# Bilinear layer: output products of two feature pairs in one PSUM group, and work moved between VectorE and GpSimd

## The chip, the cores and the metric

The kernel runs on one core of a Trainium2 chip. The metric is the time of one execution in microseconds of the device, median of three runs. Before the change it is 724.49 us (724.02 to 724.53).

## The reference

Three layers follow one another; the 1152 tokens are 2 batches of 576.

```python
# attention: 2 batches, 8 heads, 576 tokens, 64 columns a head
scores = scale * np.matmul(q, k.transpose(0, 1, 3, 2))
cum = np.cumsum(np.maximum(s, 0.0), axis=-1)
bias = -(cum[:, :, :, None] - cum[:, :, None, :])
scores = np.where(causal, -1000000000.0, scores + np.minimum(bias, 0.0))
x = softmax(scores) @ v                      # as 1152 x 512
# four experts, 512 -> 1024 -> 512, weighted by shares p
for e in range(E):
    h = np.maximum(x @ w1[e], 0.0)
    out += p[:, e:e + 1] * (h @ w2[e])
# bilinear layer, 512 -> 1536 -> 512
a = out @ w_a
b = out @ w_b
return (a * b @ w_out).astype(np.float32)
```

(The softmax is shortened here; all is float32.)

## The kernel before

**Precision.** Every float32 factor is kept as two parts: a high part, which ScalarE copies (L80), and a low part, which another engine makes by a subtraction (L81). A product is three matmuls, high by high, high by low and low by high (`mm3`, L281). In the program's names a trailing h or l is the part: `wh`, `wl` are weights, `h2h`, `h2l` the features between two layers, `tqh`, `tql` sums of input quarters.

**Stages.** To about 200 us attention runs with the first expert beside it. Then come three relu experts to about 480 us, a turn of the sum `acc` into the input `x` of the last layer, and from about 505 us the bilinear layer. Its 1536 features are worked off in six stages, m = 0 to 5, of one feature pair each (two blocks of 128). A stage multiplies the 1152 tokens by the pair's `wa` and then by its `wb`. 896 of the tokens go through `quadrants`, which forms seven products of quarters instead of eight, with sums of weight quarters (`sums`, made at L189 to L192) and of input quarters; each product is 128 x 448. The other 256 tokens go directly (`pst`). `keep_b` multiplies a by b in PSUM (L1202) and splits the result into `h2h` and `h2l`. Then the output tiles follow: nine tiles of 128 tokens by 512 columns, each six matmuls with the pair's half of `wo` (`second_pair`). The first stage copies a tile to `acc` on ScalarE (L1223), the others add it on VectorE (L1225), and the last one sends it out (L1227); the very last tile is done in two halves of 256 columns (`last_tile`, L1213).

**Weights.** `wa`, `wb` and `wo` come as 64-bit numbers. A piece is loaded by a DMA on SyncE's queue into one of three `raw` buffers and made into float32 by `narrow`: an Abs on ScalarE (L161), a max and min on GpSimd (L162), and three bit operations on VectorE (L166, L170, L174). Two such pieces make a wide pair (`tp`), one a piece of `wo` (`t`); there is one buffer of each. `split_pair` then makes the four sums on GpSimd and both low parts, of the quarters themselves (`wl<-tp`) and of the sums (`wl<-sums`), on GpSimd too, each one instruction of 128 x 1024. A wide piece of `wo` has its low part of 128 x 512 on GpSimd. For the experts' weights, which come as float32, the sums stand on VectorE and the low parts on GpSimd. Three places hold pairs, two hold halves of `wo` (or of the experts' second weights), and two pairs of `h2h`, `h2l` stand at a time.

**Order.** The program emits units of work one after another, and a clock of assumed costs says when a weight piece is loaded and split beside them; the pieces stand in a list: `wa` and `wb` of a stage with the `wo` of the stage before between them. `pipelined` lets the output tiles of a stage stand beside the products of the next. A scheduler then orders each engine's instructions by a simulated timeline; on the chip each engine works off its list in order and waits at semaphores. Products use five PSUM banks, output tiles three.

## Time and profile before

| | |
|---|---|
| time, median of three runs | 724.49 us (724.02 to 724.53) |
| profiled execution: its time, its span | 725.65 us, 723.9 us |
| TensorE matmul busy | 710.9 us, 98% of the span |
| VectorE busy | 512.9 us, 71% |
| GpSimd busy | 398.8 us, 55% |
| ScalarE busy | 323.5 us, 45% |
| TensorE's granted clock | 1.00 throughout |

A matmul's end is modelled and reaches into the next one, so the starts are the thing to read: where two of them lie further apart than the columns need, TensorE stood still. In a row of the timeline the bracket at its end is the engine's idle time before the instruction and what ended it. PE is TensorE, DVE VectorE, ACT ScalarE, POOL GpSimd, and SPq SyncE's queue that issues DMAs.

### The profile page before, as it was taken

The numbers are of one execution on the slowest core, as the hardware profiler recorded it, in microseconds if no ns is written. First come the engines' busy times: TensorE is split into PE (matmuls) and PEld (weight loads), VectorE is DVE, ScalarE is ACT, GpSimd is POOL, SyncE is SP. The second block draws the span as 40 slices with busy tenths as digits, with TensorE's granted clock in tenths as the row PEclk, the third lists the DMA queues.
The fourth block names the chain that finished last, engine by engine and source line by source line (L and its number), as shares of the span: only waits on it lengthen the run. The fifth ranks groups of instructions, "written<-read, shape, count | busy, mean of one in ns | idle before, by whom it ended". The sixth has DMA issues, their size and how long they took to land.

```text
span 723.9 us, 10979 instructions
## 1 busy us (share of the span) xinstructions
PE 710.9 (98%) x3884; PEld 620.9 (86%) x3886; DVE 512.9 (71%) x1060; ACT 323.5 (45%) x722; POOL 398.8 (55%) x329
## 2 busy tenths in 40 slices
PE   9999999999999999999999999999999999999998
PEld 5886798999899888888888888887999888888886
DVE  5586878767686866765655666589973969787674
ACT  3597899877434333331223123334544424243410
POOL 5476866655235544430333057687277879788600
PEclk9999999999999999999999999999999999999999
DMA  8665434442111211120111021222021222212003
GB/s 328 209 176 141 126 88 119 124 120 62 57 41 58 89 58 58 59 65 24 58 59 47 13 88 59 88 87 88 30 87 59 88 88 83 92 60 88 1 0 131
DMA packets 33724, 61.42 MB, mean 85 GB/s; under 512 B 3285, under 2 KB 17525, under 8 KB 33669
## 3 DMA queue, kind: packets, MB, share of 16 engines
q1 hardware_dynamic: 33189, 59.61, 26.6%
q10 hardware_dynamic: 480, 1.11, 0.4%
q8 instruction: 31, 0.51, 0.3%
q14 instruction: 24, 0.20, 0.1%
HBM read 55.11 MB, written 2.58 MB: 80 GB/s over the span
## 4 chain that ended last, share of the span: by engine, by line
PE 76%; DVE 9%; POOL 5%; issue 4%; ACT 4%; DMA 3%; SPq 0%; POOLq 0%; ACTq 0%; DVEq 0%
PE ps L281 34%; PE psq L281 24%; PE pst L281 6%; PE av L702 2%; PE tr L670 2%; POOL wl L81 2%; PE ps L1037 2%; DMA raw<-in_wo 1%; DVE el L686 1%; DVE tp L174 1%; PE lullps L736 1%; ACT e L651 1%; DVE h2l L81 1%; DVE tp L170 1%; POOL tp L162 1%
## 5 line engine op out<-in xcount | busy, mean ns | idle before, releaser
L281 PE MATMUL ps<-wh,h2h 128*128 128x512 f32 (+1 forms) x334 | 131.1, 392 | 0.6 <-ACT h2h L80 0.6
L281 PE MATMUL ps<-wl,h2h 128*128 128x512 f32 (+1 forms) x334 | 129.9, 389 | 0.0
L81 POOL TENSOR_TENSOR wl<-raw,wh 128x1024 fp32r<-128x1024 f32 x24 | 58.2, 2433 | 129.0 <-ACT wh L80 98.6
L281 PE MATMUL ps<-wh,h2l 128*128 128x512 f32 (+1 forms) x334 | 125.6, 390 | 0.0
L335 DVE SCALAR_TENSOR_TENSOR acc<-ps,pr,acc 128x512 f32<-128x512 f32 x111 | 82.3, 746 | 41.1 <-PE ps L281 40.4
L281 PE MATMUL psq<-xh,wh 128*128 128x448 f32 (+1 forms) x224 | 81.7, 365 | 0.1
L281 PE MATMUL psq<-xh,wl 128*128 128x448 f32 (+1 forms) x224 | 81.4, 363 | 0.0
L281 PE MATMUL psq<-xl,wh 128*128 128x448 f32 (+1 forms) x224 | 81.3, 363 | 0.0
L281 PEld LDWEIGHTS ps<-wh,h2l 128*128 128x128 f32 x334 | 62.7, 188 | 13.2
L281 PEld LDWEIGHTS ps<-wh,h2h 128*128 128x128 f32 x334 | 62.8, 188 | 13.0 <-ACT h2h L80 1.3
L346 ACT ACTIVATE h2h<-psq 128x448 fp32r<-128x448 f32 (+1 forms) x56 | 29.5, 530 | 95.5 <-PE psq L281 76.4
L281 PEld LDWEIGHTS ps<-wl,h2h 128*128 128x128 f32 x334 | 62.8, 188 | 10.9
L81 POOL TENSOR_TENSOR wl<-sums,wh 128x1024 fp32r<-128x1024 f32 x24 | 58.3, 2427 | 4.9 <-ACT wh L80 4.9
L80 ACT ACTIVATE wh<-raw 128x1024 fp32r<-128x1024 f32 x24 | 25.5, 1062 | 69.6 <-PE ps L281 53.0
L281 PE MATMUL psq<-tqh,wh 128*128 128x448 f32 x144 | 53.0, 368 | 1.3 <-DVE h2l L81 0.9
L281 PE MATMUL psq<-tql,wh 128*128 128x448 f32 x144 | 52.6, 365 | 0.0
L281 PE MATMUL psq<-tqh,wl 128*128 128x448 f32 x144 | 52.5, 364 | 0.0
L162 POOL TENSOR_SCALAR tp<-tp 128x512 f32<-128x512 f32 x24 | 48.0, 2017 | 5.8 <-ACT tp L161 5.8
L686 DVE TENSOR_TENSOR el<-tr,eh 128x512 fp32r<-128x512 f32 (+5 forms) x80 | 38.3, 484 | 16.4 <-ACT eh L685 15.6
L659 POOL TENSOR_SCALAR e<-e,r 128x448 f32<-128x448 f32 (+4 forms) x64 | 37.8, 595 | 17.5 <-DVE r L658 12.9
L281 PEld LDWEIGHTS psq<-xh,wh 128*128 128x128 f32 x224 | 42.1, 188 | 4.3 <-ACT s L445 0.9
L281 PEld LDWEIGHTS psq<-xl,wh 128*128 128x128 f32 x224 | 42.1, 188 | 3.5
(205 smaller groups left out, 1877.2 us busy)
## 6 DMA issues: line engine op xcount, KB each, us to landing
raw<-in_w SPq DMA_DIRECT2D x32, 512.0 KB
raw<-in_wa SPq DMA_DIRECT2D x12, 512.0 KB
raw<-in_wb SPq DMA_DIRECT2D x12, 512.0 KB
raw<-in_wo SPq DMA_DIRECT2D x12, 512.0 KB
kr<-in_kT SPq DMA_DIRECT2D x16, 288.0 KB
w<-in_w SPq DMA_DIRECT2D x8, 512.0 KB
vr<-in_v SPq DMA_DIRECT2D x16, 160.0 KB
kb<-ks SPq DMA_DIRECT2D x16, 144.0 KB
```

What stands on the lines that cost most here:

```text
L80: nc.scalar.activation(out=hi, in_=src, func=AF.Copy)
L81: lo_eng.tensor_tensor(out=lo, in0=src, in1=hi.bitcast(F32), op=ALU.subtract)
L162: nc.gpsimd.tensor_scalar(out=t.bitcast(F32), in0=t.bitcast(F32), scalar1=2.0**-15, scalar2=GMAX, op0=ALU.max, op1=ALU.min,)
L170: nc.vector.scalar_tensor_tensor(out=t, in0=lo, scalar=29, in1=t, op0=ALU.logical_shift_right, op1=ALU.bitwise_or,)
L281: ins = nc.tensor.matmul(ps, lhsT=l, rhs=r, start=first and k == 0, stop=last and k == 2, skip_group_check=more)
L335: nc.vector.scalar_tensor_tensor(out=dst, in0=ps, scalar=share, in1=dst, op0=ALU.mult, op1=ALU.add)
L346: nc.scalar.activation(out=hh, in_=src, func=AF.Relu)
L659: nc.gpsimd.tensor_scalar(out=t.e, in0=t.e, scalar1=r, scalar2=1.0, op0=ALU.mult, op1=ALU.mult)
L670: ins = nc.tensor.transpose(ps[:, c - c0, :], t.e[:, k0 : k0 + P], ident)
L686: nc.vector.tensor_tensor(out=j.el[:, c0:c1, x], in0=src, in1=hi.bitcast(F32), op=ALU.subtract)
L702: ins = nc.tensor.matmul(ps[:, o:], lhsT=j.vs[:, c, :], rhs=e[:, c, o:], start=(m == 0), stop=(m == len(mms) - 1),)
L1037: ins = nc.tensor.matmul(ps, lhsT=w, rhs=x, start=start, stop=stop)
```

## The change

It has three parts. `split` can make its low part in several slices (`less`), and GpSimd makes those of pairs and of the experts' second weights in two halves: 60 instructions of 128 x 1024 become 120 of 128 x 512. The low parts of `wo` (12 instructions of 128 x 512) and the sums of wide pairs (48 of 128 x 256) move from GpSimd to VectorE. And the output products of stages m-1 and m, m odd, are summed in PSUM: a tile is one group of twelve matmuls, with nine tiles behind every odd stage and none behind an even one. With m = 1 ScalarE copies a tile to `acc`, with m = 3 and 5 VectorE adds it, so that of 44 additions of 512 columns 17 are left. The order of tiles is 7, 8, 0 to 6, and the last one is done in two halves. In the list of pieces the two `wo` of a couple of stages now stand together, between `wa` and `wb` of the next even stage.

```diff
@@ split
-    def split(hi, lo, src, lo_eng):
+    def split(hi, lo, src, lo_eng, parts=1):
         nc.scalar.activation(out=hi, in_=src, func=AF.Copy)
-        lo_eng.tensor_tensor(out=lo, in0=src, in1=hi.bitcast(F32), op=ALU.subtract)
+        less(lo, src, hi, lo_eng, parts)
+
+    def less(lo, src, hi, eng, parts):
+        n = lo.shape[1] // parts
+        for k in range(parts):
+            x = slice(k * n, k * n + n)
+            eng.tensor_tensor(out=lo[:, x], in0=src[:, x], in1=hi[:, x].bitcast(F32), op=ALU.subtract)
@@ split_pair, split_piece
-        split(*direct, r.rearrange("p c (i f) -> p i c f", i=2), nc.gpsimd)
-        split(wh[:, 8:], wl[:, 8:], sums, nc.gpsimd)
+        split(*direct, r.rearrange("p c (i f) -> p i c f", i=2), nc.gpsimd, 2)
+        split(wh[:, 8:], wl[:, 8:], sums, nc.gpsimd, 2)
...
-            split(wh[:, j, :], wl[:, j, :], t.bitcast(F32), nc.gpsimd)
+            split(wh[:, j, :], wl[:, j, :], t.bitcast(F32), nc.vector)
         elif form == "half":
-            split(wh, wl, r, nc.gpsimd)
+            split(wh, wl, r, nc.gpsimd, 2)
...
-                split_pair(key, t.bitcast(F32), nc.gpsimd)
+                split_pair(key, t.bitcast(F32), nc.vector)
@@ the list of pieces
-    for m in range(NTH * NPR):
-        queue_pair(("wa", m), wa[m // NPR], m % NPR, True)
         if m:
-            queue_half(("wo", m - 1), wo[(m - 1) // NPR], (m - 1) % NPR, True)
-        queue_pair(("wb", m), wb[m // NPR], m % NPR, True)
-    queue_half(("wo", m), wo[m // NPR], m % NPR, True)
+    for m in range(0, NTH * NPR, 2):
+        queue_factor("wa", wa, m)
+        if m:
+            queue_out(m - 2)
+            queue_out(m - 1)
+        queue_factor("wb", wb, m)
+        queue_factor("wa", wa, m + 1)
+        queue_factor("wb", wb, m + 1)
+    queue_out(m)
+    queue_out(m + 1)
@@ ab_stage
+        both = (m - 1, m)
+        order = [7, 8, *range(7)]
+
+        def products(ps, t, n):
+            for k, (mo, i) in enumerate((mo, i) for mo in both for i in range(2)):
+                mm3(
+                    ps, cols(hts["g", mo], i, slice(t, t + P)), cols(slabs["wo", mo], i, n),
+                    k == 0, k == 3,
+                )
...
         def tile_of(t):
+            last = (m, t) == (NTH * NPR - 1, order[-1] * P)
+            for n in (slice(0, DM // 2), slice(DM // 2, DM)) if last else (slice(0, DM),):
+                ps = ps_m.tile([P, n.stop - n.start], F32, tag="mm", name="ps2")
+                products(ps, t, n)
                 dst = acc[:, t // P, n]
+                if m == 1:
+                    nc.scalar.activation(out=dst, in_=ps, func=AF.Copy)
+                else:
+                    nc.vector.tensor_tensor(out=dst, in0=ps, in1=dst, op=ALU.add)
+                if m == NTH * NPR - 1:
+                    nc.sync.dma_start(out=out[t : t + P, n], in_=dst)
...
-        o = [(("wo", m), T1, lambda t=t: tile_of(t)) for t in range(0, NT, P)]
+        keys = tuple(("wo", mo) for mo in both)
+        o = [(keys, 2 * T1, lambda t=t * P: tile_of(t)) for t in order] if m % 2 else []
```

In the rows of the changed program a line of the kernel stands six or more lines further down: L81 has become L87, L162 L168, L166 L172, L170 L176, L174 L180, L189 to L192 L195 to L198, L281 L287, L436 L442, and L1202 L1218.

**GpSimd, in the third stage.** Before, one wide pair with the piece of `wo` and the next pair's first two pieces behind it:

```order
L162 TENSOR_SCALAR tp<-tp 128x512 x2
L190 TENSOR_TENSOR sums<-tp 128x256
L189 TENSOR_TENSOR sums<-tp 128x256
L191 TENSOR_TENSOR sums<-sums,tp 128x256
L81 TENSOR_TENSOR wl<-tp,wh 128x1024
L192 TENSOR_TENSOR sums<-tp,sums 128x256
L162 TENSOR_SCALAR t<-t 128x512
L81 TENSOR_TENSOR wl<-sums,wh 128x1024
L162 TENSOR_SCALAR tp<-tp 128x512 x2
```

After the change; the first `t<-t` here is the one whose shift stands second in VectorE's list below:

```order
L168 TENSOR_SCALAR tp<-tp 128x512 x2
L87 TENSOR_TENSOR wl<-tp,wh 128x512 x2
L87 TENSOR_TENSOR wl<-sums,wh 128x512 x2
L168 TENSOR_SCALAR t<-t 128x512
L168 TENSOR_SCALAR tp<-tp 128x512 x2
L168 TENSOR_SCALAR t<-t 128x512
L87 TENSOR_TENSOR wl<-tp,wh 128x512 x2
L87 TENSOR_TENSOR wl<-sums,wh 128x512 x2
```

The sums are gone from here, each subtraction stands as two halves, and the halves of the quarters and of the sums stand one behind the other, four in a row, with no other instruction between them. The max and min of a piece of `wo` stood between the two subtractions of a pair; now it stands behind all four halves.

**VectorE, in the third stage, at the split of the 256 direct tokens (`h2l<-pst`).** Before:

```order
L1202 TENSOR_TENSOR pst<-pst,sr 128x512
L1202 TENSOR_TENSOR psq<-psq,u_6208 128x448
L166 TENSOR_SCALAR t<-t 128x512
L81 TENSOR_TENSOR h2l<-pst,h2h 128x2x256
L170 SCALAR_TENSOR_TENSOR t<-raw,t 128x512
L81 TENSOR_TENSOR h2l<-psq,h2h 128x448
L174 SCALAR_TENSOR_TENSOR t<-raw,t 128x512
L436 TENSOR_TENSOR psq<-psq,s_6409 128x448
L1202 TENSOR_TENSOR psq<-psq,s_6206 128x448
L166 TENSOR_SCALAR tp<-tp 128x512
L436 TENSOR_TENSOR psq<-psq,u_6410 128x448
L170 SCALAR_TENSOR_TENSOR tp<-raw,tp 128x512
```

After:

```order
L442 TENSOR_TENSOR psq<-psq,u_6417 128x448
L172 TENSOR_SCALAR t<-t 128x512
L1218 TENSOR_TENSOR pst<-pst,sr 128x512
L1218 TENSOR_TENSOR psq<-psq,u_6182 128x448
L176 SCALAR_TENSOR_TENSOR t<-raw,t 128x512
L172 TENSOR_SCALAR tp<-tp 128x512
L87 TENSOR_TENSOR h2l<-pst,h2h 128x2x256
L442 TENSOR_TENSOR psq<-psq,s_6415 128x448
L180 SCALAR_TENSOR_TENSOR t<-raw,t 128x512
L87 TENSOR_TENSOR h2l<-psq,h2h 128x448
L176 SCALAR_TENSOR_TENSOR tp<-raw,tp 128x512
L442 TENSOR_TENSOR psq<-psq,u_6416 128x448
```

A shift that waits for GpSimd (L166 before, L172 after) stands ahead of `h2l<-pst` in both. After the change it is one of `tp`, and a bit operation and a shift more stand between the product `pst<-pst,sr` and `h2l<-pst`.

**TensorE, an output tile of the last stage.** Before, one tile (`ps2_7460` is its PSUM tile, `h2h_7322` and `h2l_7323` the features of the last pair, `wh_3501` and `wl_3502` the buffers that hold `wo`):

```order
L281 MATMUL ps2_7460<-wh_3501,h2h_7322 128x512
L281 MATMUL ps2_7460<-wl_3502,h2h_7322 128x512
L281 MATMUL ps2_7460<-wh_3501,h2l_7323 128x512
L281 MATMUL ps2_7460<-wh_3501,h2h_7322 128x512
L281 MATMUL ps2_7460<-wl_3502,h2h_7322 128x512
L281 MATMUL ps2_7460<-wh_3501,h2l_7323 128x512
```

After, one tile:

```order
L287 MATMUL ps2_7448<-wh_3501,h2h_7105 128x512
L287 MATMUL ps2_7448<-wl_3502,h2h_7105 128x512
L287 MATMUL ps2_7448<-wh_3501,h2l_7106 128x512
L287 MATMUL ps2_7448<-wh_3501,h2h_7105 128x512
L287 MATMUL ps2_7448<-wl_3502,h2h_7105 128x512
L287 MATMUL ps2_7448<-wh_3501,h2l_7106 128x512
L287 MATMUL ps2_7448<-wh_3501,h2h_7346 128x512
L287 MATMUL ps2_7448<-wl_3502,h2h_7346 128x512
L287 MATMUL ps2_7448<-wh_3501,h2l_7347 128x512
L287 MATMUL ps2_7448<-wh_3501,h2h_7346 128x512
L287 MATMUL ps2_7448<-wl_3502,h2h_7346 128x512
L287 MATMUL ps2_7448<-wh_3501,h2l_7347 128x512
```

The first six of its twelve matmuls take the features of the pair before (`h2h_7105`, `h2l_7106`), the last six those of the last pair; one addition to `acc` follows instead of two.

## Rows read from the trace of the kernel before

**Rows 1.** The page's busy time: us, share of the span, instructions of each engine.

```profile
PE 710.9 (98%) x3884; PEld 620.9 (86%) x3886; DVE 512.9 (71%) x1060; ACT 323.5 (45%) x722; POOL 398.8 (55%) x329
```

**Rows 2.** Stretches: length, then busy us and instructions of each engine, clock, DMA.

```profile
300.00:360.00 60.00, 60.00 (x300) 52.49 (x299) 37.77 (x63) 16.54 (x25) 21.47 (x9) 1.00 0.17 53
597.50:635.00 37.50, 36.37 (x189) 31.32 (x187) 30.43 (x47) 13.15 (x22) 31.63 (x21) 1.00 0.27 85
```

**Rows 3.** Timeline, 599 to 603 us: start, duration, engine, line, operation, [idle <-releaser].

```profile
599.45 2.40 POOL L81 TENSOR_TENSOR wl<-sums,wh 128x1024 fp32r<-128x1024 f32 x1
...
600.50 1.64 DVE L166 TENSOR_SCALAR t<-t 128x512 int32<-128x512 int32 x1
...
601.83 0.37 PE L281 MATMUL psq<-xl,wh 128*128 128x448 f32 x1
...
602.04 0.37 PE L281 MATMUL psq<-xh,wl 128*128 128x448 f32 x1
602.06 0.68 DVE L81 TENSOR_TENSOR h2l<-pst,h2h 128x512 fp32r<-128x512 f32 x1
...
602.88 0.45 PE L281 MATMUL psq<-tqh,wh 128*128 128x448 f32 x1 [0.47 <-DVE h2l L81]
```

**Rows 4.** Timeline 630 to 636 us, all engines.

```profile
630.38 0.28 PE L281 MATMUL pst<-xh,wl 128*128 128x256 f32 x1
...
630.51 0.34 SPq L156 DMA_DIRECT2D raw<-in_wo  x1
...
631.04 0.47 PE L281 MATMUL psq<-tqh,wh 128*128 128x448 f32 x1 [0.38 <-DVE u L436]
...
634.25 0.66 ACT L161 ACTIVATE t<-raw 128x512 f32<-128x512 f32 x1 [2.71 <-DMA raw<-in_wo]
...
634.41 0.37 PE L281 MATMUL psq<-xh,wl 128*128 128x448 f32 x1
...
635.40 0.49 PE L281 MATMUL ps<-wh,h2h 128*128 128x512 f32 x1 [0.62 <-ACT h2h L80]
```

**Rows 5.** Timeline 638 to 641 us, VectorE and TensorE.

```profile
638.24 1.42 DVE L166 TENSOR_SCALAR t<-t 128x512 int32<-128x512 int32 x1
...
639.82 0.37 PE L281 MATMUL psq<-xh,wl 128*128 128x448 f32 x1
...
640.41 0.44 PE L281 MATMUL psq<-tqh,wh 128*128 128x448 f32 x1 [0.22 <-DVE h2l L81]
```

**Rows 6.** Timeline 673 to 677 us, ScalarE and TensorE.

```profile
673.93 1.06 ACT L80 ACTIVATE wh<-sums 128x1024 fp32r<-128x1024 f32 x1 [2.58 <-POOL sums L192]
...
674.90 0.58 ACT L80 ACTIVATE h2h<-pst 128x512 fp32r<-128x512 f32 x1
...
675.80 0.37 PE L281 MATMUL psq<-xh,wl 128*128 128x448 f32 x1
...
676.35 0.44 PE L281 MATMUL psq<-tqh,wh 128*128 128x448 f32 x1 [0.18 <-DVE h2l L81]
```

**Rows 7.** Lines by shape, 510 to 724 us: busy us, mean ns, idle.

```profile
L1225 DVE TENSOR_TENSOR acc<-ps,acc 128x512 f32<-128x512 f32 x44 | 29.3, 683 | 8.5 <-PE ps L281 8.3
...
L81 POOL TENSOR_TENSOR wl<-t,wh 128x512 fp32r<-128x512 f32 x10 | 15.0, 1495 | 20.2 <-ACT wh L80 20.2
...
L166 DVE TENSOR_SCALAR t<-t 128x512 int32<-128x512 int32 x9 | 8.1, 895 | 1.1 <-POOL t L162 1.0
```

**Rows 8.** Single lines: shortest, median, longest ns; first and last start; shape.

```profile
L81 POOL TENSOR_TENSOR wl<-t,wh x10: 1293/1312/2020, 516.7 to 683.9; 128x512 fp32r<-128x512 f32 x10
...
L166 DVE TENSOR_SCALAR t<-t x9: 411/804/1700, 522.3 to 679.4; 128x512 int32<-128x512 int32 x9
...
L190 DVE TENSOR_TENSOR sums<-raw x12: 409/418/2626, 200.2 to 399.4; 128x256 f32<-128x256 f32 x12
L190 POOL TENSOR_TENSOR sums<-tp x12: 732/782/1296, 428.7 to 665.6; 128x256 f32<-128x256 f32 x12
...
L227 DVE TENSOR_TENSOR wl<-raw,wh x8: 679/688/1811, 46.7 to 111.2; 128x512 fp32r<-128x512 f32 x8
```

More of the change, by code (lines that the diff above doesn't have):

```diff
@@ L1009, in fused_kernel, with queue_factor, queue_out @@
     queue_half(("v2", ex, m), w2[2 * ex + m // NPR], m % NPR)
-    for m in range(NTH * NPR):
-        queue_pair(("wa", m), wa[m // NPR], m % NPR, True)
-        if m:
-            queue_half(("wo", m - 1), wo[(m - 1) // NPR], (m - 1) % NPR, True)
-        queue_pair(("wb", m), wb[m // NPR], m % NPR, True)
-    queue_half(("wo", m), wo[m // NPR], m % NPR, True)
+    def queue_factor(n, w, m):
+        queue_pair((n, m), w[m // NPR], m % NPR, True)
+    def queue_out(m):
+        queue_half(("wo", m), wo[m // NPR], m % NPR, True)
+    for m in range(0, NTH * NPR, 2):
+        queue_factor("wa", wa, m)
+        if m:
+            queue_out(m - 2)
[5 more added lines that the diff above has]
+    queue_out(m + 1)
     def time_of(n, k):
@@ L1205, in keep_b, with tile_of @@
             hts["g", m] = hs[0]
-        def last_tile(t):
-            for n in (slice(0, DM // 2), slice(DM // 2, DM)):
-                ps = ps_m.tile([P, DM // 2], F32, tag="mm", name="ps2")
-                for i in range(2):
-                    mm3(ps, cols(hts["g", m], i, slice(t, t + P)), cols(slabs["wo", m], i, n), i == 0, i == 1)
-                dst = acc[:, t // P, n]
-                nc.vector.tensor_tensor(out=dst, in0=ps, in1=dst, op=ALU.add)
-                nc.sync.dma_start(out=out[t : t + P, n], in_=dst)
-        def tile_of(t):
-            if (m, t) == (NTH * NPR - 1, NT - P):
-                last_tile(t)
-                return
-            ps = second_pair(("g", m), slabs["wo", m], t)
-            dst = acc[:, t // P, :]
-            if m == 0:
-                nc.scalar.activation(out=dst, in_=ps, func=AF.Copy)
-            else:
-                nc.vector.tensor_tensor(out=dst, in0=ps, in1=dst, op=ALU.add)
-            if m == NTH * NPR - 1:
-                nc.sync.dma_start(out=out[t : t + P, :], in_=dst)
-        o = [(("wo", m), T1, lambda t=t: tile_of(t)) for t in range(0, NT, P)]
+        both = (m - 1, m)
[6 more added lines that the diff above has]
+                )
+        def tile_of(t):
+            last = (m, t) == (NTH * NPR - 1, order[-1] * P)
+            for n in (slice(0, DM // 2), slice(DM // 2, DM)) if last else (slice(0, DM),):
+                ps = ps_m.tile([P, n.stop - n.start], F32, tag="mm", name="ps2")
+                products(ps, t, n)
+                dst = acc[:, t // P, n]
+                if m == 1:
[6 more added lines that the diff above has]
+        o = [(keys, 2 * T1, lambda t=t * P: tile_of(t)) for t in order] if m % 2 else []
         ua = quadrants(("wa", m), QB, keep_a, False, m == 0)
```

## Prediction

> **What bounds the kernel now.** I read the page's busy times first. TensorE matmuls are busy 710.9 of 723.9 us, 98%, VectorE 71%, GpSimd 55% [rows 1]. So only TensorE's idle time can be won, and only in a stretch where it has some. The table of stretches shows where. Through the relu experts, 300 to 360 us, TensorE is busy 60.00 of 60 us; in the third feature pair of the bilinear part, 597.5 to 635 us, 36.37 of 37.50, with VectorE at 30.43 and GpSimd at 31.63, both over 80% [rows 2]. All three parts of the change act in or near that last part, and what they can win is its few stalls.
>
> Then the timeline at each stall. The distance between two matmul starts is the measure, since ends are modelled: a 448-column matmul follows another after 0.21 us (601.83 to 602.04), a 256-column one after 0.12, which is the same scaled by width. What exceeds that is a stall.
>
> - 602.04 to 602.88 us: 0.84, so a stall of 0.63. TensorE waits for `h2l` on VectorE, whose subtraction gives a PSUM bank back. It began at 602.06 because the shift before it (L166) took 1.64 us instead of 0.41 [rows 3, 8]; beside it runs GpSimd's 128x1024 subtraction, from 599.45 for 2.40 us, and the shift ends only after that does.
> - 639.82 to 640.41: 0.59, a stall of 0.38, with the same shift at 1.42 us [rows 5].
> - 630.38 to 631.04: 0.66, a stall of 0.54, for a VectorE sum that comes late in a full queue [rows 4].
> - 634.41 to 635.40: 0.99, a stall of 0.78. The ScalarE copy `h2h` stands behind an Abs (634.25) that waited 2.71 us for a piece of `wo`, whose DMA was issued at 630.51 [rows 4].
> - 675.80 to 676.35: 0.55, a stall of 0.34. ScalarE's `h2h` (674.90) stands behind `wh<-sums`, which waited 2.58 us for the last of GpSimd's pair sums [rows 6].
>
> Together 0.63 + 0.38 + 0.54 + 0.78 + 0.34 = 2.67 us: the prize.
>
> **The change part by part.**
>
> GpSimd's 128x1024 subtractions in halves. A whole one takes 2.40 us [rows 3], one of 128x512 a median of 1312 ns [rows 8], so a pair of halves costs 0.2 us more on GpSimd, sixty times 0.2 = 12 us in all. What it is worth lies on VectorE: a shift that meets a whole subtraction is held up to 2.4 us, one that meets a half up to 1.3 and half of that on average, if the engine lets VectorE in between the two. In the two places of rows 3 and 5 the hold was 1.64 - 0.41 = 1.23 and 1.42 - 0.41 = 1.01; at 0.65 each they fall by 0.58 and 0.36, which takes 0.58 of the 0.63 and 0.36 of the 0.38. With chance in who meets whom I book -0.7 of 1.01.
>
> Four halves can now stand in a row, since the pair sums no longer stand between them on GpSimd. VectorE's next shift needs a GpSimd max/min that is queued behind them: 4 x 1.3 = 5.2 us before that max/min starts, instead of 2 x 2.4 + 0.78 = 5.6. That is no worse.
>
> Pair sums on VectorE, and `wo`'s low parts. A sum (128x256) takes 418 ns on VectorE against 782 on GpSimd [rows 8], so the chain of four is 4 x 0.36 = 1.5 us shorter; the 0.34 at 675.80 sat behind it and goes, -0.34. VectorE gets 48 x 0.42 = 20.2 us over the kernel and, at 0.69 each as in the early weights [rows 8], 12 x 0.69 = 8.3 us for `wo`. GpSimd loses 48 x 0.78 = 37 us of sums and 12 x 1.31 = 16 us of `wo`, and is some 40 us lighter with its halves.
>
> Output tiles of two pairs in one PSUM group. 27 additions to `acc` at 683 ns [rows 7] go: -18.4 us on VectorE. So VectorE's load is up by 20.2 + 8.3 - 18.4 = 10.1 us overall. In the bilinear part, for two stages: 2 x 30.43 = 60.9 before; less nine additions (6.1), plus 16 sums (6.7) and four `wo` pieces (2.8), 64.3 of 75.0 us, from 81% to 86%. The matmuls stay the same, but that the last tile's 512 columns are cut in two for twelve products instead of six: six more instructions at some 0.01, +0.04. The path behind the last matmul is unchanged.
>
> What moves is where the output tiles stand. Before, each stage has nine tiles of 6 x 0.23 us beside its products, time in which TensorE works and VectorE need only add. Now TensorE runs two stages, about 2 x (37.5 - 12.4) = 50 us, with no finished tile between, and VectorE has to keep a product in front of every matmul there.
>
> The queue of `wo`. Both pieces of two pairs now stand together, long before they are used. The 0.78 at 634.41 came of one piece asked for too late and an Abs in front of `h2h`; with ScalarE reaching that Abs later against the DMA's issue it goes, -0.78. Where a new order puts an Abs in front of another copy with the DMA still under way, it returns.
>
> The stall at 630.38 comes of a full VectorE; I book half, -0.27.
>
> The new cost is VectorE in the dense 50 us. No row shows it. Lower bound: nothing, as VectorE has 86% of the work time and runs ahead. Upper bound: in each of the three dense stretches one hold by a half, mean 1.50 us [rows 7], falls on TensorE in full, 4.5 us. I take 0.4, nearer to nothing, since the stalls of rows 3 and 5 show that a hold of 1.0 to 1.2 us reaches TensorE with a third to a half of itself and twice in the part; so one such stall comes back.
>
> The page "SBUF — State Buffer" of the Trainium skill, section "Who interferes with whom", says that a VectorE instruction with two SBUF inputs contends with a GpSimd instruction that reads SBUF, and that the loser is blocked for the whole instruction. It speaks against the second part: sums and `wo` subtractions have two SBUF inputs. The trace agrees where such a sum stood on VectorE, 409 ns at best and 2626 at worst [rows 8]. By the rule, each of the 60 added instructions can be held for a half, and the sum would be the second rival's; by the rows, where GpSimd's sums and subtractions were such instructions before as well, it is mine.
>
> Sum: -0.7 - 0.34 - 0.78 - 0.27 + 0.04 + 0.4 = -1.65 us against the profiled execution's 725.65, so 724.0. That execution was 1.16 above the median of 724.49; the same step from the median gives **722.8 us**.
>
> **The rivals.**
>
> 1. Nothing is won in sum. TensorE is 98% busy, and a stall that goes leaves the next late engine close behind: VectorE at 86%, the turn ahead of the bilinear part with sums now in VectorE's queue. For it: VectorE and GpSimd are both over 80% in rows 2, so each stall has neighbours. Against: three of the five stalls have one clear cause that the change takes away. Of the 2.09 us booked as gain 1.6 come back as other stalls: 724.49 - 2.09 + 1.6 + 0.04 = 724.0.
> 2. Slower: VectorE is held in the dense stretch. Place: the second half of each even stage and the odd one behind it, three times. Mechanism: shifts, sums and `wo` subtractions meet GpSimd's halves; VectorE falls behind and TensorE finds no free PSUM bank. Price: a hold of 1.50 per stretch in full, 3 x 1.50 = 4.5; 724.49 - 2.09 + 0.04 + 4.5 = 726.9. It decides once VectorE's slack in a stretch, 50 us less 86%, some 7 us, is eaten by holds, five of 1.5. For it: `t`'s shift has a mean of 895 ns [rows 7] where the shortest took 411 [rows 8]. Against: halves shorten each hold.
> 3. Full gain. All five stalls go and nothing comes: 724.49 - 2.67 + 0.04 = 721.9, and up to 1 us less if small stalls that I have not listed go too. For it: GpSimd is relieved by some 40 us. Against: VectorE is not.
> 4. The change doesn't do what it says: halves stand back to back on GpSimd, and VectorE doesn't get in between. Then the 0.7 stays: 724.49 - 1.65 + 0.7 = 723.5.
>
> **How the numbers follow.** Forecast 0.40, the first rival 0.20, the second 0.20, the third 0.10, the fourth 0.10. Two executions of this kernel can be told apart from about 0.2% on, 1.45 us: below 723.04 is faster, above 725.94 slower. The forecast lies just on the faster side, so its 0.40 splits into 0.28 faster, 0.10 same and 0.02 slower; the first rival's 0.20 into 0.06, 0.13 and 0.01; the second's 0.20 into 0.03 same and 0.17 slower; the third's 0.10 is all faster; the fourth's 0.10 splits into 0.04, 0.05 and 0.01. Faster is 0.28 + 0.06 + 0.10 + 0.04 = 0.48, same 0.10 + 0.13 + 0.03 + 0.05 = 0.31, slower 0.02 + 0.01 + 0.17 + 0.01 = 0.21. The range runs from the third rival's lower end, 720.9, to just short of the second's 726.9: 726.0. The forecast's own range is 721.7 to 723.9.
>
> **What would show it.** Right: `t`'s shift with a worst case near 1.7 - 1.1 = 0.6 to 1.3 us; no matmul waits for `wh<-sums` or for a DMA of `wo`; distances of starts of at most 0.4 us over a step between 515 and 700; TensorE above 36.8 of 37.5 us in the stretches of rows 2. Wrong: VectorE above 90% in the first half of the dense stretches with TensorE waiting for `h2l` or `u` there; an idle TensorE at the turn near 512 us; halves that run back to back while a shift stands longer than 1.3 us; or a time below 721, which would mean that the change acts outside the bilinear part.

## The result

The changed kernel takes 730.94 us in the median of seven runs (726.86 to 734.64), the kernel before 724.29 (724.02 to 724.53): ratio 1.0081, interval 1.0062 to 1.0100 (the two medians alone give 1.0092). It is slower by 0.8%, where 722.8 and at most 726.0 were forecast. Its profiled execution took 731.34 us with a span of 729.6 us.

The page's busy time of the changed kernel, against [rows 1]:

```profile
PE 712.8 (98%) x3890; PEld 624.8 (86%) x3892; DVE 519.0 (71%) x1093; ACT 324.4 (44%) x722; POOL 350.2 (48%) x329
```

TensorE has 1.9 us more of busy time in a span that is 5.7 us longer. VectorE has 6.1 us more, GpSimd 48.6 us less, where 10.1 more and some 40 less had been worked out. So GpSimd was relieved as forecast, and the time did not follow.

Stretches of the changed kernel (length, busy us of PE, PEld, DVE, ACT and POOL, granted clock, DMA share, GB/s):

```profile
590.00:600.00 10.00, 9.73 (x58) 8.71 (x56) 7.33 (x12) 4.84 (x8) 9.06 (x7) 1.00 0.18 59
597.50:635.00 37.50, 35.04 (x182) 31.65 (x182) 33.19 (x60) 14.42 (x24) 19.53 (x12) 0.95 0.26 85
600.00:610.00 10.00, 7.81 (x37) 7.17 (x38) 10.00 (x20) 3.81 (x8) 3.84 (x2) 0.83 0.34 105
670.00:680.00 10.00, 6.93 (x23) 5.63 (x23) 9.04 (x14) 3.26 (x5) 5.02 (x5) 0.70 0.16 49
```

The row of 597.5 to 635 us answers to the second of [rows 2]: TensorE 35.04 of 37.50 us instead of 36.37. Two things are new. TensorE is idle for 2.19 us in 600 to 610 and for 3.07 in 670 to 680, and the granted clock there, 1.00 everywhere before, is 0.83 and 0.70, that is, part of the stretch at the lower of the two levels, 1.2 GHz. Between these places TensorE is busy without a break.

The first place, in the timeline (start, duration, engine, line, operation, idle before and releaser):

```profile
589.78 1.06 ACT L80 ACTIVATE wh<-tp 128x1024 fp32r<-128x1024 f32 x1 [4.53 <-DVE tp L180]
...
590.92 2.73 POOL L87 TENSOR_TENSOR wl<-tp,wh 128x512 fp32r<-128x512 f32 x2 [4.07 <-ACT wh L80]
...
591.05 1.44 DVE L198 TENSOR_TENSOR sums<-tp,sums 128x256 f32<-128x256 f32 x1
...
593.67 2.55 POOL L87 TENSOR_TENSOR wl<-sums,wh 128x512 fp32r<-128x512 f32 x2
...
596.19 1.92 POOL L168 TENSOR_SCALAR t<-t 128x512 f32<-128x512 f32 x1
...
598.14 0.82 DVE L172 TENSOR_SCALAR t<-t 128x512 int32<-128x512 int32 x1 [1.12 <-POOL t L168]
...
598.88 0.69 DVE L1218 TENSOR_TENSOR pst<-pst,sr 128x512 f32<-128x512 f32 x1
...
599.37 0.37 PE L287 MATMUL psq<-xh,wl 128*128 128x448 f32 x1
...
600.02 1.09 DVE L176 SCALAR_TENSOR_TENSOR t<-raw,t 128x512 int32<-128x512 int32 x1
...
601.37 0.68 DVE L87 TENSOR_TENSOR h2l<-pst,h2h 128x512 fp32r<-128x512 f32 x1
...
602.19 0.62 PE L287 MATMUL psq<-tqh,wh 128*128 128x448 f32 x1 [2.46 <-DVE h2l L87]
...
602.99 0.57 PE L287 MATMUL psq<-tqh,wl 128*128 128x448 f32 x1
```

Read it from the end. TensorE starts a matmul at 599.37 and the next at 602.19, 2.82 us apart, a stall of 2.6. It waited for `h2l`, which VectorE began at 601.37. Ahead of that stands a shift of a piece of `wo` (L172, 598.14), for which VectorE idled 1.12 us until GpSimd's max and min of 596.19. That one stood behind four halves, 590.92 to 596.22. Nor was VectorE short of time just ahead of the stall: in 590 to 600 us it was busy 7.33 of 10 us. Behind the stall the distances of starts are 0.37 us (602.62, 602.99, 603.36 and so on) until 605.60, where [rows 3] have 0.21.

The second place begins with a DMA. First what leads up to it, then the stall:

```profile
663.23 6.00 SPq L162 DMA_DIRECT2D raw<-in_wo  x3
...
667.51 0.67 ACT L167 ACTIVATE t<-raw 128x512 f32<-128x512 f32 x1 [3.62 <-DMA raw<-in_wo]
...
668.26 2.36 POOL L168 TENSOR_SCALAR t<-t 128x512 f32<-128x512 f32 x1 [4.29 <-ACT t L167]
```

```profile
670.59 2.69 POOL L87 TENSOR_TENSOR wl<-tp,wh 128x512 fp32r<-128x512 f32 x2
670.65 1.50 DVE L172 TENSOR_SCALAR t<-t 128x512 int32<-128x512 int32 x1 [1.81 <-POOL t L168]
...
671.31 0.37 PE L287 MATMUL psq<-xh,wl 128*128 128x448 f32 x1
...
672.62 0.94 DVE L195 TENSOR_TENSOR sums<-tp 128x256 f32<-128x256 f32 x1
...
674.09 0.61 DVE L442 TENSOR_TENSOR u<-psq,s 128x448 f32<-128x448 f32 x1
...
674.75 0.74 PE L287 MATMUL psq<-tqh,wh 128*128 128x448 f32 x1 [3.07 <-DVE u L442]
```

ScalarE's Abs of a piece of `wo` waited 3.62 us for its DMA, GpSimd's max and min came behind it, VectorE's shift (670.65) idled 1.81 us for that and was then held, 1.50 us, beside GpSimd's half of 670.59; then a sum was held as well (0.94). TensorE started at 671.31 and 674.75, 3.44 us apart, a stall of 3.2.

The sum closes on this. From the last transposition of the turn to the last matmul, the kernel before takes 213.4 us (507.10 to 720.48) and the changed one 220.1 (506.11 to 726.21), +6.7; it is 1.0 us ahead when it gets there. The stalls are 2.6 + 3.2 = 5.8. The slow steps cost 1.6 (nine steps in 3.41 us at 0.205 each) and 2.9 (eight of 448 columns and seven of 512 in 6.10 us, where 3.23 would do), 4.5 in all. The old stalls are gone, -2.67 for the five of [rows 3 to 6] and some 0.4 for smaller ones. 5.8 + 4.5 - 3.1 = 7.2, half a microsecond above the measured 6.7.

### The profile page after: what moved, and what is told of

Same layout as the page of the kernel before. It is cut to its first block, busy times and chain, and to the rows that moved or that the text cites. A ratio compares the mean times of both kernels' runs of the same rounds, so it can differ in the third digit from the quotient of the medians.

```text
span 729.6 us, 11028 instructions
## 1 busy us (share of the span) xinstructions
PE 712.8 (98%) x3890; PEld 624.8 (86%) x3892; DVE 519.0 (71%) x1093; ACT 324.4 (44%) x722; POOL 350.2 (48%) x329
## 4 chain that ended last, share of the span: by engine, by line
PE 73%; POOL 7%; DVE 6%; DMA 5%; ACT 4%; issue 4%; SPq 0%; ACTq 0%; POOLq 0%; DVEq 0%
PE ps L287 33%; PE psq L287 26%; PE pst L287 6%; POOL wl L87 3%; PE av L708 2%; PE tr L676 2%; PE ps L1053 2%; POOL tp L168 1%; DMA va<-in_v 1%; POOL t L168 1%; ACT e L657 1%; DVE el L692 1%; PE sc L634 1%; PE sc L633 1%; DVE tp L180 1%
## 5 line engine op out<-in xcount | busy, mean ns | idle before, releaser
L287 PE MATMUL ps<-wl,h2h 128*128 128x512 f32 (+1 forms) x336 | 130.9, 390 | 0.0
L287 PE MATMUL ps<-wh,h2h 128*128 128x512 f32 (+1 forms) x336 | 130.6, 392 | 0.0
L287 PE MATMUL ps<-wh,h2l 128*128 128x512 f32 (+1 forms) x336 | 128.6, 389 | 0.0
L87 POOL TENSOR_TENSOR wl<-raw,wh 128x512 fp32r<-128x512 f32 x48 | 62.3, 1325 | 135.2 <-ACT wh L80 114.8
L287 PE MATMUL psq<-xh,wh 128*128 128x448 f32 (+1 forms) x224 | 82.0, 366 | 0.0
L287 PE MATMUL psq<-xl,wh 128*128 128x448 f32 (+1 forms) x224 | 81.6, 364 | 0.0
L287 PE MATMUL psq<-xh,wl 128*128 128x448 f32 (+1 forms) x224 | 81.6, 364 | 0.0
L287 PEld LDWEIGHTS ps<-wh,h2l 128*128 128x128 f32 x336 | 63.3, 188 | 13.0
L287 PEld LDWEIGHTS ps<-wl,h2h 128*128 128x128 f32 x336 | 63.6, 189 | 11.2
L287 PEld LDWEIGHTS ps<-wh,h2h 128*128 128x128 f32 x336 | 63.5, 189 | 11.2
L87 POOL TENSOR_TENSOR wl<-sums,wh 128x512 fp32r<-128x512 f32 x48 | 62.2, 1319 | 19.9 <-ACT wh L80 13.6
L287 PE MATMUL psq<-tqh,wh 128*128 128x448 f32 x144 | 53.7, 374 | 5.5 <-DVE u L442 3.1
L287 PE MATMUL psq<-tql,wh 128*128 128x448 f32 x144 | 53.4, 371 | 0.0
L287 PE MATMUL psq<-tqh,wl 128*128 128x448 f32 x144 | 53.3, 370 | 0.0
L87 POOL TENSOR_TENSOR wl<-tp,wh 128x512 fp32r<-128x512 f32 x24 | 32.1, 1360 | 41.3 <-ACT wh L80 41.3
L168 POOL TENSOR_SCALAR tp<-tp 128x512 f32<-128x512 f32 x24 | 46.1, 1938 | 9.2 <-ACT tp L167 9.2
L168 POOL TENSOR_SCALAR t<-t 128x512 f32<-128x512 f32 x12 | 23.8, 1985 | 46.8 <-ACT t L167 46.8
```

Of the source, the lines that this page charges most:

```text
L87: eng.tensor_tensor(out=lo[:, x], in0=src[:, x], in1=hi[:, x].bitcast(F32), op=ALU.subtract)
L168: nc.gpsimd.tensor_scalar(out=t.bitcast(F32), in0=t.bitcast(F32), scalar1=2.0**-15, scalar2=GMAX, op0=ALU.max, op1=ALU.min,)
L287: ins = nc.tensor.matmul(ps, lhsT=l, rhs=r, start=first and k == 0, stop=last and k == 2, skip_group_check=more)
```

## The experiments

Ratios are to the kernel before on the same chip, whose median was 725.13 us for e1 to e4, 725.03 for e5 to e8, 724.10 for e9 to e12 and 724.19 for e13 to e15. Line numbers shift by a few from kernel to kernel.

**First four: which part does it.** The theory to begin with, the order theory, was that two `wo` worked off back to back put late shifts into VectorE's list. The rival, the load theory, was that VectorE has too much to do.

e1, the kernel before with the halves and with VectorE's new work, its tiles and list left as they were:

```diff
-        split(wh[:, 8:], wl[:, 8:], sums, nc.gpsimd)
+        split(wh[:, 8:], wl[:, 8:], sums, nc.gpsimd, 2)
...
-            split(wh[:, j, :], wl[:, j, :], t.bitcast(F32), nc.gpsimd)
+            split(wh[:, j, :], wl[:, j, :], t.bitcast(F32), nc.vector)
...
-                split_pair(key, t.bitcast(F32), nc.gpsimd)
+                split_pair(key, t.bitcast(F32), nc.vector)
```

> The changed kernel with its output tiles and its list of weight pieces as before: halves on GpSimd, pair sums and the low parts of wo on VectorE, but a group of tiles behind every stage and one piece pair of wo a stage. Order theory (the two long stalls come from VectorE standing at a shift of a piece of wo that is late, because the two wo of a couple of stages are worked off back to back): no stall above 1 us in the bilinear part, clock 1.00, 722 to 724.5 us. Load theory (VectorE simply has too much to do between the output tiles): VectorE is 18 us heavier than in the changed kernel, so long stalls stay or grow, clock below 1.00, 730 us or more.

728.90 us, ratio 1.0050 (1.0035 to 1.0065). The old list alone does not give 724: the order theory's forecast failed. There are stalls of 0.95 and 0.84 us at the turn and one of 2.0 near 674 us, the latter with VectorE busy all of the time and a lower clock:

```profile
670.00:680.00 10.00, 8.18 (x35) 6.77 (x34) 10.00 (x18) 4.51 (x7) 3.06 (x3) 0.89 0.15 52
```

That is what the load theory says, at less than its price of 730 us. Four of the ten executions of e1 have a mean clock of 1.000 and take 726.6 to 729.0 us, so the clock is not most of its loss.

e2, the other way round, the kernel before with the tiles of two pairs and the new list alone:

```diff
+            queue_out(m - 2)
+            queue_out(m - 1)
...
-        o = [(("wo", m), T1, lambda t=t: tile_of(t)) for t in range(0, NT, P)]
+        o = [(keys, 2 * T1, lambda t=t * P: tile_of(t)) for t in order] if m % 2 else []
```

> The kernel before with the output tiles of two pairs in one PSUM group and the new list of pieces alone: sums and low parts stay on GpSimd in whole instructions. Order theory: the pieces of wo stand back to back here too, so at least one stall above 2 us and a granted clock below 1.00, 726 to 734 us. Load theory: VectorE has 18 us less to do than before and none of the added sums, so at most the old stalls, 722 to 724 us, clock 1.00.

735.88 us, ratio 1.0136 (1.0115 to 1.0157), the slowest of all, with matmul starts 4.45 and 3.45 us apart at 601 and 644 us. VectorE has 18 us less to do here than in the kernel before. So load alone is not it either; the part on tiles and list does the harm by itself. At 601 us TensorE waits for `h2l` on VectorE, but at 644 us for the weights of `wo` themselves: the matmul at 647.53 is a tile's, and it had waited 3.09 us for ScalarE's `wh`, which stood behind a bit operation on `t` that took VectorE 2.75 us beside a whole subtraction of GpSimd.

e3, the changed kernel with GpSimd's subtractions whole:

```diff
-        split(*direct, r.rearrange("p c (i f) -> p i c f", i=2), nc.gpsimd, 2)
-        split(wh[:, 8:], wl[:, 8:], sums, nc.gpsimd, 2)
+        split(*direct, r.rearrange("p c (i f) -> p i c f", i=2), nc.gpsimd)
+        split(wh[:, 8:], wl[:, 8:], sums, nc.gpsimd)
```

> The changed kernel with GpSimd's subtractions whole again (128x1024). Order theory: a whole pair of subtractions takes 4.8 us where four halves take 5.3, so the stalls stay, 728 to 733 us. Load theory with GpSimd's lock as the cause: holds up to 2.4 us instead of 1.3, so it is slower than the changed kernel, 732 us or more.

734.58 us, ratio 1.0118 (1.0096 to 1.0140): 0.4% above the changed kernel, though the two intervals still touch. The halves seem to be worth something here, and the long stalls (2.6 and 4.1 us) stand at the same two places.

e4, the changed kernel with sums and low parts of `wo` on GpSimd again:

```diff
-            split(wh[:, j, :], wl[:, j, :], t.bitcast(F32), nc.vector)
+            split(wh[:, j, :], wl[:, j, :], t.bitcast(F32), nc.gpsimd)
...
-                split_pair(key, t.bitcast(F32), nc.vector)
+                split_pair(key, t.bitcast(F32), nc.gpsimd)
```

> The changed kernel with the sums of wide pairs and the low parts of wo on GpSimd again. Order theory: the long stalls depend on which VectorE instruction stands behind the late shift; the shift of the first wo piece stands elsewhere here, so one of the two stalls goes, 724 to 729 us. Load theory: VectorE is 28 us lighter, no long stall, clock 1.00, 721 to 723.5 us.

726.77 us, ratio 1.0019 (1.0007 to 1.0031). Moving the work back gives 0.6% of the 0.8% back; five stalls of 0.3 to 1.5 us are left. It fell inside the order theory's range and not the load theory's; neither had named these stalls. e4 also differs from e2 in the halves alone, 1.0019 against 1.0136: with the new list and the work on GpSimd they are worth 1.2%.

**Second four: the late shift, the list, the clock.**

e5, the changed kernel with the max and min of `wo` on VectorE, so that its shifts wait for GpSimd no more (`eng` is `nc.gpsimd` otherwise):

```diff
-            narrow(t, r[:, :, 0], r[:, :, 1])
+            narrow(t, r[:, :, 0], r[:, :, 1], nc.vector)
```

> The changed kernel with the max and min of the pieces of wo (12 instructions of 128x512) on VectorE instead of GpSimd, so that no shift of a piece of wo waits for GpSimd any more; VectorE gets some 12 x 0.6 = 7 us more to do. Order theory: the stall near 599 us, whose chain runs through four halves and the max and min on GpSimd, goes with its slow-clock stretch; the one near 671 us, which begins with a late DMA of wo, may stay; 724 to 728 us. Load theory: more load on VectorE, so longer stalls, 732 us or more.

728.54 us, ratio 1.0050 (1.0032 to 1.0067), between the ranges of the two theories. The wait for GpSimd is gone and the long stall near 599 us is not; the one near 671 us, which was allowed to stay, has shrunk to stalls of 0.8 and 0.7 us. Near 599 us:

```profile
588.48 2.73 POOL L87 TENSOR_TENSOR wl<-tp,wh 128x512 fp32r<-128x512 f32 x2 [3.67 <-ACT wh L80]
588.56 1.50 DVE L197 TENSOR_TENSOR sums<-sums,tp 128x256 f32<-128x256 f32 x1
...
590.09 1.41 DVE L198 TENSOR_TENSOR sums<-tp,sums 128x256 f32<-128x256 f32 x1
...
594.29 1.40 DVE L172 TENSOR_SCALAR t<-t 128x512 int32<-128x512 int32 x1
...
599.40 0.48 PE L287 MATMUL psq<-tqh,wh 128*128 128x448 f32 x1 [2.06 <-DVE u L442]
```

VectorE reaches the place late all the same, and beside GpSimd's halves it is held: two sums take 1.50 and 1.41 us, which take 0.42 unhindered, and the shift 1.40 instead of 0.41. So the late shift is one way of making VectorE late, not the cause of the stall. TensorE's starts are 2.43 us apart there.

e6, the changed kernel with the old list of pieces:

```diff
-    for m in range(0, NTH * NPR, 2):
+    for m in range(NTH * NPR):
         queue_factor("wa", wa, m)
         if m:
-            queue_out(m - 2)
             queue_out(m - 1)
         queue_factor("wb", wb, m)
-        queue_factor("wa", wa, m + 1)
-        queue_factor("wb", wb, m + 1)
     queue_out(m)
-    queue_out(m + 1)
```

> The changed kernel with the list of weight pieces as it was before (one wo between wa and wb of each stage), output tiles of two pairs kept. Theory that the two wo standing back to back make the pieces late: no DMA of wo is waited for in front of a stall, 723 to 727 us. Theory that the cover is what is missing (no output tile to multiply while VectorE works at weights in the even stage): stalls above 2 us stay in even stages, 729 us or more.

724.79 us, ratio 0.9989 (0.9963 to 1.0014). This edit alone takes the whole loss back, and it is 0.6% faster than e1, which has the same list, halves and work on VectorE with the old tiles. The forecast that stalls stay because an even stage has no tile, 729 us or more, failed. From 520 us to the end no stall is longer than 0.51 us. What is left are two stalls of 0.95 and 0.84 us at the turn, the second of them here, where an even start-to-start of 0.12 becomes 0.96:

```profile
514.58 0.28 PE L287 MATMUL pst<-xh,wl 128*128 128x256 f32 x1
...
515.54 0.39 PE L287 MATMUL pst<-xh,wh 128*128 128x256 f32 x1 [0.69 <-ACT sr L1207]
```

e7 and e8, the kernel before with five or three multiplications by 1.0 more on VectorE, to make one stall of a known size:

```diff
             nc.vector.tensor_tensor(out=src, in0=src, in1=sa[i, at_(x)], op=ALU.mult)
+            for _ in range(5 if (m, i) == (2, None) else 0):      # e8: 3
+                nc.vector.tensor_scalar(out=src, in0=src, scalar1=1.0, scalar2=None, op0=ALU.mult)
```

> The kernel before with five more multiplications by 1.0 on VectorE in PSUM at the 256 direct tokens of the third stage, 5 x 0.69 = 3.4 us in front of the h2l that TensorE waited 0.63 us for. If a long stall lowers TensorE's clock: one stall of 3 to 4 us near 602 us, followed by matmuls at 0.37 us a step instead of 0.20, and 727 us or more, above the 3.5 us that the stall by itself adds. If the clock in the changed kernel fell for another reason: clock 1.00 throughout and 726 to 728 us.

> As the run with five, with three such multiplications, 3 x 0.69 = 2.1 us: a stall of 2 to 2.7 us. If any stall of this kind lowers the clock, the steps behind it are 0.37 us; if only a longer one does, they stay at 0.20 and the time is 725 to 727 us.

726.46 us, ratio 1.0023 (1.0000 to 1.0046), and 727.14, ratio 1.0033 (1.0017 to 1.0048). They did not do what they were to do: in both, three stalls of 1.4, 1.0 and 0.8 us came in place of one, presumably because the scheduler reckons with the added work and arranges the engines anew. What they show is that these together, 3.2 us, left the clock alone in the profiled execution (e7):

```profile
600.00:610.00 10.00, 7.33 (x33) 5.45 (x32) 10.00 (x17) 3.29 (x6) 7.39 (x5) 1.00 0.15 52
```

**Third four: the list again, and a better kernel.**

e9 is e2 with the old list, the same edit as in e6.

> The run with the output tiles of two pairs alone (e2), with the list of weight pieces as before. Theory of the list (four pieces of wo one behind the other are what makes VectorE stand, whatever else is changed): the two stalls of 4.5 and 3.5 us go, clock 1.00, 723 to 727 us. Theory of the missing cover (pairs alone leave TensorE without tiles in the even stage): one stall above 2 us at least, 730 us or more.

724.82 us, ratio 1.0008 (0.9992 to 1.0025), against 1.0136 of e2. The list takes the loss back a second time, without halves and without work moved to VectorE, and again the forecast by missing tiles, 730 us or more, failed. Seven stalls of 0.25 to 1.0 us are left, none longer.

e10, the changed kernel with the two `wo` apart: `wa(m)`, `wo(m-2)`, `wb(m)`, `wo(m-1)`, `wa(m+1)`, `wb(m+1)`.

```diff
         if m:
             queue_out(m - 2)
-            queue_out(m - 1)
         queue_factor("wb", wb, m)
+        if m:
+            queue_out(m - 1)
```

> The changed kernel with the second wo of each couple moved behind wb in the list: wa(m), wo(m-2), wb(m), wo(m-1), wa(m+1), wb(m+1). Theory that four pieces one behind the other are too many: no long stall, 722 to 725 us, clock 1.00. Theory that it matters when a wo is asked for rather than how many stand together: the second wo still meets the stage without tiles, at least one stall above 1.5 us, 726 us or more.

730.53 us, ratio 1.0091 (1.0076 to 1.0106), as slow as the changed kernel. It does not separate the two theories. The edit spreads the pieces inside the loop alone; the last two `wo` still stand together at the end of the list, and the one long stall, 4.94 us between two starts at 671 us, lies behind them. At the first place, where the pieces do stand apart, the longest stall is 1.2 us instead of 2.6, and there TensorE waits for the weights of `wo`:

```profile
652.07 17.66 SPq L162 DMA_DIRECT2D raw<-in_wo  x4
```

```profile
603.86 0.37 PE L287 MATMUL psq<-xh,wl 128*128 128x448 f32 x1
605.24 0.73 PE L287 MATMUL ps<-wh,h2h 128*128 128x512 f32 x2 [1.01 <-ACT wh L80]
```

So both may count: that four pieces stand together, and when a `wo` is asked for. How much later that is, the queue of SyncE shows; in the changed kernel (start, time to the end of the last one's issue, and the number of issues):

```profile
576.86 10.89 SPq L162 DMA_DIRECT2D raw<-in_wa  x2
589.75 21.21 SPq L162 DMA_DIRECT2D raw<-in_wo  x4
615.96 9.39 SPq L162 DMA_DIRECT2D raw<-in_wb  x2
```

and in e12, which has the old list:

```profile
557.41 10.66 SPq L162 DMA_DIRECT2D raw<-in_wo  x2
...
584.99 3.27 SPq L162 DMA_DIRECT2D raw<-in_wa  x2
591.07 15.04 SPq L162 DMA_DIRECT2D raw<-in_wo  x2
```

The pieces that come with the fifth stage's `wa` in the changed kernel at 589.75 are `wo` of the third and fourth stage; with the old list `wo` of the third stage is issued at 557.41 us, 32 us and so most of a stage earlier. A tile of two pairs can be opened with its first six products as soon as the even pair's `wo` and features are there. With the old list `wo` is there by the time the even stage's features are.

e11, e6 with sums and low parts on GpSimd (the edit of e4), and e12, e6 with those of the first stages alone:

```diff
-            split(wh[:, j, :], wl[:, j, :], t.bitcast(F32), nc.vector)
+            split(wh[:, j, :], wl[:, j, :], t.bitcast(F32), nc.gpsimd if key[1] < 1 else nc.vector)
...
-                split_pair(key, t.bitcast(F32), nc.vector)
+                split_pair(key, t.bitcast(F32), nc.gpsimd if key[1] < 2 else nc.vector)
```

> The run with the old list (e6), with the pair sums and the low parts of wo on GpSimd again: halves and output tiles of two pairs are what is left of the change. If the stalls of 0.95 and 0.84 us at the turn in e6 come from the sums that VectorE got: they go, and with no other stall the time is 722 to 723.5 us. If the sums on GpSimd bring the old stalls of the kernel before back: 724 to 726 us.

> The run with the old list (e6), with the sums of the first two stages and the low parts of the first wo on GpSimd, the rest on VectorE. If the stalls at the turn come from VectorE's added work there: they go (0.95 + 0.84 us), 722 to 723.5 us, faster than the kernel before and than e6. If the schedule merely shifts: 724 to 726 us.

e11: 723.23 us, ratio 0.9993 (0.9981 to 1.0006); the stalls at the turn are gone, and one of 1.5 us is there at 630. It differs from e9 in the halves alone, and the intervals of the two overlap. e12: 722.04 us, ratio 0.9977 (0.9965 to 0.9990). It beats both kernels, by 2.1 us the one before. The stalls at the turn are gone with it and one of 0.98 us at 597.84 is all that is left above 0.2.

**Last three: cover.** In e12 TensorE has products of tiles between 600 and 608 us. The tile products by the first of their three kinds, 584 to 612 us, in the changed kernel (shortest, median, longest ns; first and last start):

```profile
L287 PE MATMUL ps<-wh,h2h x3: 390/393/398, 607.5 to 607.9; 128*128 128x512 f32 x3
```

and in e12:

```profile
L287 PE MATMUL ps<-wh,h2h x6: 387/390/395, 600.4 to 607.5; 128*128 128x512 f32 x6
```

The cover theory in a new form, made after e6 and e9 had refuted the first one: the new list does harm because these come too late to fill TensorE's time while VectorE works at weights. e13 takes them away under the old list; a tile that takes the odd pair first can't be opened early.

```diff
-        both = (m - 1, m)
+        both = (m, m - 1)
```

> The fastest run so far (e12), with the two pairs of a tile multiplied in the other order, the odd pair first: a tile can then not be opened before the odd stage is done, and TensorE has no tile products of the even pair to put between the products near 600 and 672 us. Cover theory (the old list helps because wo of the even pair is there a stage earlier, so that opened tiles fill TensorE's time while VectorE works at weights): stalls above 1.5 us come near 600 and 672 us, 725 us or more. Order theory (the old list helps because fewer pieces of wo stand in VectorE's way): no change, 721.5 to 723 us.

727.27 us, ratio 1.0040 (1.0025 to 1.0055), against 0.9977 of e12. The stall at 671 us is back, and the low clock with it (the two starts, then the stretch):

```profile
671.04 0.37 PE L287 MATMUL psq<-tqh,wl 128*128 128x448 f32 x1
...
673.47 0.65 PE L287 MATMUL psq<-tqh,wh 128*128 128x448 f32 x1 [2.06 <-DVE h2l L87]
```

```profile
670.00:680.00 10.00, 7.90 (x29) 6.58 (x30) 8.32 (x16) 4.98 (x9) 1.91 (x1) 0.83 0.00 1
```

In e12 the same stretch, and the one that answers to [rows 2]:

```profile
597.50:635.00 37.50, 36.69 (x196) 33.01 (x195) 34.96 (x63) 15.70 (x26) 22.36 (x15) 1.00 0.24 85
670.00:680.00 10.00, 10.00 (x51) 8.84 (x50) 7.42 (x14) 3.39 (x6) 1.92 (x1) 1.00 0.00 0
```

VectorE is busier in e12 than in the changed kernel, 34.96 us of 37.50 instead of 33.19, and TensorE waits less. At 600 us e13 has a stall of 0.8 only; of the two places forecast, one came.

e14 is the same edit under the new list.

> The changed kernel with the odd pair first in each tile. Cover theory: the tiles opened early there come after the stalls anyway (7 tile products from 677.15 us on, the stall being at 671.3), so nothing is gained and the cover that is left goes as well: 729 to 736 us. Order theory: the same, 728 to 733 us, so this run only tells whether the order of the pairs costs something by itself.

727.49 us, ratio 1.0043 (1.0028 to 1.0058), faster than the changed kernel and below both expectations. There is a longest stall of 2.3 us, at 598.66, with four of 0.9 to 1.3 us between 591 and 630, and none above 0.25 us near 671, although this kernel has the new list and no tile opened early. The clock stays up:

```profile
590.00:600.00 10.00, 8.18 (x50) 7.25 (x48) 6.30 (x12) 3.97 (x7) 8.05 (x5) 1.00 0.15 54
600.00:610.00 10.00, 7.72 (x46) 7.03 (x47) 10.00 (x18) 3.78 (x6) 4.65 (x3) 1.00 0.30 106
```

e15 is e12 with GpSimd's subtractions whole.

> The fastest run so far (e12) with GpSimd's subtractions whole again (128x1024). If the halves are worth what was forecast for them (0.7 us of holds): 722.5 to 724 us. If with the old list the holds are covered by tiles: the same as e12, 721.5 to 722.5 us. If whole ones hold VectorE long enough for a long stall as in e3: 725 us or more.

724.55 us, ratio 1.0003 (0.9993 to 1.0013), against 0.9977: above the range of the first guess. Whole subtractions bring two stalls of 1.2 and 1.4 us.

## Why the prediction was wrong

Step by step, as it was put.

- "Both pieces of two pairs now stand together, long before they are used." This is the step that failed. The second half is true of the tiles' last products and false of their first: for the even pair the new list brings `wo` most of a stage later than the old one (589.75 us against 557.41). The stall for which I booked -0.78 did go, but the new list had a cost that was no term of the sum: undoing it alone is worth 0.9% (e6) and 1.3% (e9 against e2) of the time. How it costs this is shown only in part: under the old list the early tile products decide over the long stall at 671 us (e12 against e13), not over the one at 600.
- "The new cost is VectorE in the dense 50 us", upper bound 4.5 us, 0.4 taken. The place was right, but the size was not: 5.8 us of stalls and 4.5 of slow clock, in two stretches. The 86% that made me take so little is a mean over 75 us, tiles included; without the nine additions, 64.3 - 6.1 = 58.2 us of VectorE's work stand against the dense 50 us (an estimate from the prediction's own terms), unless part of it is done beside the tiles. Nor does the load by itself decide: in e12 VectorE is busy 93% and TensorE hardly stalls. That it matters whether TensorE has a tile open when VectorE is late fits e12 and e13, and not e14. And I priced a stall by one hold, where several holds and a wait add up (at the second place a wait of 1.81 us, a shift at 1.50 instead of 0.41 and a sum at 0.94 instead of 0.42).
- The clock was no term of the sum. 4.5 us of the loss are matmuls at the lower level behind the two stalls. The kernel before has no stall above 0.8 us in the bilinear part, so no row of it showed this.
- "Four halves can now stand in a row ... no worse", 5.2 us instead of 5.6. Wrong, and the rows of the order showed it: before, the max and min stood between the two subtractions, behind one whole one and a sum, 2.4 + 0.8 = 3.2 us. After, it started 5.3 us behind the first half. e5 shows that this wait alone isn't the stall.
- The halves, -0.7. Right in sign, too small: e12 against e15 gives 0.26%, 1.9 us, the changed kernel against e3 0.37%, 2.7 us, e4 against e2 1.17%, 8.5 us; only e11 against e9 shows no clear difference. The longest shift of a piece of `wo` still takes 1.5 us, where at most 1.3 was named as a sign of being right:

```profile
L172 DVE TENSOR_SCALAR t<-t x11: 414/420/1509, 521.6 to 691.2; 128x512 int32<-128x512 int32 x11
```

- Sums on VectorE, -0.34, and `wo`'s low parts. The stall behind `wh<-sums` went. But e4 shows that under the new list the move costs 0.6%, and e6 that it brings 1.8 us of stalls at the turn, which rival 1 had named and the sum had not. In e5 two such sums took 1.50 and 1.41 us instead of 0.42 beside GpSimd's halves. The Trainium skill, "SBUF — State Buffer", section "Who interferes with whom", states that such a sum contends with GpSimd's reads; the trace agrees. The prediction left that to a rival.
- VectorE's additions and shifts behave as priced, against [rows 7]:

```profile
L1242 DVE TENSOR_TENSOR acc<-ps,acc 128x512 f32<-128x512 f32 x17 | 11.4, 687 | 14.3 <-PE ps L287 14.3
...
L87 DVE TENSOR_TENSOR wl<-t,wh 128x512 fp32r<-128x512 f32 x12 | 8.5, 709 | 0.7 <-ACT wh L80 0.7
...
L172 DVE TENSOR_SCALAR t<-t 128x512 int32<-128x512 int32 x11 | 7.7, 699 | 4.8 <-POOL t L168 4.8
```

The five old stalls of [rows 3 to 6] all went, also the one at 630 of which I had kept half, so the gain was there: 2.67 us and a bit. Of the rivals the second came nearest, with its place and its sign, but at 726.9 us it was 4 us short, and I gave it 0.20. The fourth did not come: at the second place the shift ended at 672.15 us, while GpSimd's second half still ran to 673.28, so VectorE did get in between two halves.

What stays open is the cause behind the list: how much of the two stalls is the missing tile, how much the order on VectorE, and how much `wo` itself coming late, for which TensorE waits directly in e2 and e10. Every edit lets the scheduler arrange the engines anew, and no run changes the early tiles with that order held. That e14 was faster than the changed kernel, without its stall near 671 us, is explained by neither theory. e6 against the changed kernel (the list alone) and e13 against e12 (the order of products alone) are as near as these runs come.

## What to carry to other kernels

Where TensorE waits for another engine, count also what it could do meanwhile at that place, and not the other engine's load alone: output tiles that can be opened early may be cover, and a list that brings their weights most of a stage later may take it away. When several edits come together, undo each by itself first; here undoing the list took back the whole loss, and the rest, kept off the turn, was a gain of 0.2%. It is not so that the other parts are harmless each by itself: halves and work on VectorE under the old tiles cost 0.5% (e1). And read an order for what stands ahead of each waiting instruction now and before, both times to the end.

## What the runs showed of the hardware

In the bilinear part the granted clock fell to the lower level only behind a long stall of TensorE: behind matmul starts 2.19 us apart (e1), 2.43 (e5, e13), 2.82 and 3.44 (the changed kernel), 2.82 and 4.30 (e3), 3.45 and 4.45 (e2) and 4.94 (e10). It was 1.00 throughout behind 1.57, 1.21 and 0.99 in a row (e7), and once behind 2.50 us (e14). That gives no limit, for in attention it fell in the profiled executions of some kernels with the same distances at which it stayed in others. Between 70 and 80 us the starts lie at most 1.39 us apart in the kernel before and in e11 alike (before, then e11; e4 and e15 have 0.83 there too):

```profile
70.00:80.00 10.00, 8.83 (x42) 5.96 (x43) 7.61 (x25) 9.21 (x27) 8.49 (x9) 1.00 0.71 211
```

```profile
70.00:80.00 10.00, 8.83 (x37) 6.34 (x36) 7.14 (x23) 7.62 (x24) 8.50 (x9) 0.83 0.71 214
```

While it was down a step of 448 columns took 0.37 us instead of 0.205, nine steps behind the first stall of the changed kernel, and fifteen steps were slow behind the second. The spread of the time goes with it: seven executions of the changed kernel go from 726.86 us with a mean clock of 0.998 to 734.64 with 0.991. Seven of the kernel before stay within 0.5 us, but beside e1 to e4 some of the same kernel took 726.5 to 727.2 us with 0.997 or 0.998.

A VectorE instruction beside a GpSimd subtraction can take several times as long as alone: a sum of 128x256 1.50 us instead of 0.42 beside a half (e5), a bit operation of 128x512 2.75 us instead of 0.68 beside a whole one (e2).
